# New planner constants for the issue order of a fused attention and MLP kernel on one core

## The chip, the cores and the metric

The kernel runs on one core of a Trainium2 chip. Its engines are TensorE (PE in the profile, its weight loads PEld), VectorE (DVE), ScalarE (ACT), GpSimd (POOL) and SyncE (SP), which only issues DMA transfers here. The metric is the device time of one execution in microseconds, lower is better. A run is one timed execution; the median of three is given.

## The reference

Causal attention in a window of 128 positions, with a linear bias per head, over 8 batches of 576 positions with 8 heads of 64; then an MLP with a rational activation on the 4608 x 512 result. All inputs are f32, but the two weight matrices of the MLP are float64.

```
scores = q @ k.T / 8 - slope[h] * (i - j)   where 0 <= i - j < 128, else -1e9
x = softmax(scores) @ v                     # (4608, 512)
h = x @ w_in                                # (4608, 2048), w_in and w_out are float64
g = (a0 + a1 h + a2 h^2 + a3 h^3) / (1 + |b0| |h| + |b1| h^2 + 1e-6)
out = g @ w_out                             # (4608, 512)
```

## The kernel before

The 4608 rows are cut into 36 blocks of 128, and these into 18 tiles of two blocks. For each tile there are two attention jobs `j` (tile `j // 2`, four heads each), so 36 jobs. A job's PE block holds the value matmuls of the job before it and its own scores: `attention(j)` emits `values(j - 1)` and `scores` as one step from job 3 on. After the scores come, for each of two head pairs, a predicated copy that folds the band (line 491), bias and minimum (532), exponentials (537), sums and reciprocals (544, 545), the scaling (546, on GpSimd), a transposition (on PE at 561 for the first six jobs, by a DMA transposition at line 568 with ScalarE copies at 566 and 569 on either side for the others), and two GpSimd steps on the far part (589, 590; the first jobs have VectorE and ScalarE steps at 580 to 582 in their place). `out_values` then makes `x_hi` and `x_lo`, the two parts of the MLP's input.

The MLP of a tile, `mlp(t, cs)`, runs over 16 chunks `c` of 128 hidden units, two at a time: up-projection into PSUM `h` (line 667), the rational function on ScalarE, GpSimd and VectorE (lines 681 to 707), and the down-projection into two accumulators (line 724), which also wait for the tile before to be copied out (752). Tiles 1 to 17 multiply with weights and inputs split into a high and a low part, three matmuls for each product. Tile 0 multiplies with unsplit f32 weights.

The weights arrive as 64-bit words. `convert(k)` loads a chunk of 512 KB of `w_in` (even k) or `w_out` (odd k), and turns it into f32 in three steps (628 on ScalarE, 629 on ScalarE or VectorE, 630 on VectorE). `split(c, m)` makes the high part on ScalarE (642) and the low part on GpSimd or VectorE (643), when the loads that share the high part's memory have been converted. PSUM has four buffers with the tag `h`, which the up-projections, the score blocks' sides and the conversions share.

No step is issued where it stands in the source. Each is handed to `Plan.op` with a due time, a cost per engine it can run on, its reads and writes, and perhaps a time `after` which the plan may place it. `Plan.order` goes through a planned time line: whenever an engine is free in the plan, it takes from the steps that are ready there the one with the lowest due time. The sequence in which steps are taken is then the order of the instructions on each engine and on SP's DMA queue. On the chip an engine only follows its sequence and waits on semaphores; due times, costs and `after` have no effect there other than through the order. `LATENCY` and the slack (SP, SV, SA, SG, in us for PE, VectorE, ScalarE and GpSimd) lengthen planned waits between engines. A step marked `sb` is planned to exclude such steps between VectorE and GpSimd.

The due times come from some 40 constants:

- `m_time(t, c)`: the up-projection of a chunk. Tile 0 starts at T0 and lasts L0, later blocks last L1 each. Down-projections are due ML later (LL more in the last tile), elementwise steps ME later.
- `a_time(j)`: jobs 0 and 1 at A0 and A0 + 4 DA; job 2 at B2, job 3 at B3; later ones at `m0 + (j % 2 + AOFF) * (m1 - m0) * ZA / 2`, where m0 and m1 are the starts of the tile before and of the job's own. Loads of kq are due JL before, those of v VL after kq; AW is how much ahead the plan may place them. V0, D0, D2, D4, DU, BL and DL shift steps within a job, VE the v loads of the first jobs.
- `c_time(k)`: conversions, C0 + DC c for w_in and CO + DO c for w_out; the load is due WL before.
- splits: S0 + DS (2c + m), in the plan not before SL ahead of that.
- FE ends the PE's warming matmuls (line 760) that fill its idle time at the start. OE shifts the output copy.

Of the kernel before, what the change touches and what calls it, by code (L numbers as in the profile page):

```python
# [16 lines left out]
U16 = mybir.dt.uint16  # L17
# [4 lines left out]
P = 128  # L22
# [259 lines left out]
def banded_attention_ratio_mlp(ctx: ExitStack, tc: tile.TileContext, kqv, w_in, w_out, ab, bias, ident, out):  # L282
    nc = tc.nc
# [10 lines left out]
    NJ = 2 * NTILE  # L294


    A0, DA, T0, L0, L1 = -20.125, 1.042, 19.836, 59.132, 26.846
    AOFF, D2, D3, JL, VL = -0.9676, 4.293, 7.221, 11.472, 6.149
    SP, SV, SA, SG, LL = 0.000768, 0.2712, 0.1218, 0.4427, 2.857
    ML, ZA, ME, OE, C0 = 24.839, 1.199, 1.338, 10.451, 0.4053  # L300
    DC, CO, DO, WL, S0 = 3.813, 18.57, 3.877, 4.536, 80.884
    DS, SL, AW, BL, VE = 1.477, 8.756, 26.824, 0.9349, 13.143
    DU, V0, DL, B2, B3 = 0.7375, 2.733, 1.877, 23.544, 56.47
    FE, D0, D4 = 19.023, 0.5665, 1.663

    plan = Plan({"p": 1000 * SP, "v": 1000 * SV, "a": 1000 * SA, "g": 1000 * SG})

    def slot(pool, shape, dtype, name, tag=None, view=None):
        return Slot(pool, count[id(pool)], shape, dtype, name, tag or name, view)

    def ap(s):
        if s.ap is None:
            s.ap = s.pool.tile(s.shape, s.dtype, name=s.name, tag=s.tag)
        return s.ap

    def act(n, psum, ptr=0):
        return (67 if psum else 105) + 0.833 * n + 95 * ptr

    def dve(n, ptr=0):
        return 69 + 1.042 * n + 60 * ptr  # L320
# [42 lines left out]
    def a_time(j):  # L363

        t = j // 2
        if t == 0:
            return A0 + 4 * DA * j
        if t == 1:
            return B2 if j == 2 else B3
        m0, m1 = m_time(t - 1, 0), m_time(t, 0)  # L370
        return m0 + (j % 2 + AOFF) * (m1 - m0) * ZA / 2
# [5 lines left out]
    def job(j, i):  # L377

        t, p = j // 2, 2 * (j % 2) + i
        W = tile_width(2)  # L380
        N = 5 * P
        u0 = a_time(j) + i * DL
        o = (t * NPAIR + p) * P * W
        src = kqv[o : o + P * W].rearrange("(q w) -> q w", w=W)
        kq = slot(sb4, [P, 5 * P], F32, "kq")
        v = slot(sb6, [P, 2, 2, P], F32, "v")
        late = 0.0 if t == 0 else 1000 * (u0 - AW)

        def load_v(e, b):
            part = src[:, N + b * P : N + (b + 2) * P]  # L390
            eng[e].dma_start(ap(v)[64 * b : 64 * b + 64].rearrange("r g j c -> r g (j c)"), part.rearrange("(g r) w -> r g w", g=2))

        plan.op(u0 - JL if t else 2 * j + i - 19, {"s": 1150}, lambda e: eng[e].dma_start(ap(kq), src[:, :N]), writes=[(kq, 0)], after=late)
        for b in range(2):
            plan.op(u0 - JL + VL if t else 2 * j + i - VE, {"s": 560}, lambda e, b=b: load_v(e, b), writes=[(v, b)], after=late, rows=0.5)
        kt = lambda b: ap(kq)[:, b * P : (b + 2) * P]
        qt = lambda b: ap(kq)[:, (3 + b) * P : (4 + b) * P]
        return kt, qt, v, [(kq, 0)]
# [40 lines left out]
    def attention(j):  # L439

        A = a_time(j)
        t = j // 2
        back = j - 1 if j > 2 else None
        if j != 1:
            shared[:] = [slot(ps4, [P, 2, 2, P], F32, f"side{h}", tag="h") for h in range(2)]
        side, n = list(shared), 1 if j == 1 else 0
        if j == 1:
            banks = [slot(ps1, [P, 2, 2, P], F32, f"sc{h}", tag=f"acc{h}") for h in range(2)]
            main, mk = (lambda h: ap(banks[h])), [(banks[0], 0), (banks[1], 0)]
        elif j < NJ:  # L450
            sc = slot(ps1, [P, 2, 2, 2, P], F32, "sc")
            main, mk = (lambda h: ap(sc)[:, h]), [(sc, 0), (sc, 1)]
        extra = lambda h: ap(side[h])[:, n].rearrange("q i (b c) -> q i b c", b=2)
        if j < NJ:
            jobs = [job(j, i) for i in range(2)]

        def scores(i):
            kt, qt = jobs[i][:2]
            for b in range(2):
                for part in range(2):  # L460
                    for g in range(2):
                        for h in range(2):
                            r, c = slice(64 * h, 64 * h + 64), slice(64 * g, 64 * g + 64)
                            k0 = P * g if part == 0 else P - 64 * g
                            to = extra(h)[c, i, b] if part else main(h)[c, i, b]
                            nc.tensor.matmul(to, qt(b)[r, c], kt(b)[r, k0 : k0 + (64 if part else P)], start=True, stop=True, tile_position=(64 * h, 64 * g))  # L466

        beside = lambda b: ap(side[b])[:, 1]
        if t == 0:
            for i in range(2):  # L470
                plan.op(A + DU * i, {"p": 290 + 664}, lambda e, i=i: scores(i), reads=jobs[i][3], writes=mk + [(side[0], n), (side[1], n)], rows=0.9)
        else:
            small, reads, writes, cost = [], [], [], 290
            if back is not None:
                small.append(values(back, beside))
                reads += stage[back, 0][1] + stage[back, 1][1]
                writes += [(side[0], 1), (side[1], 1)]
                cost += 2 * 664 + 53
            if j < NJ:
                small += [lambda: scores(0), lambda: scores(1)]  # L480
                reads += jobs[0][3] + jobs[1][3]
                writes += mk + [(side[0], 0), (side[1], 0)]
                cost += 2 * 664
            plan.op(A, {"p": cost}, lambda e: [f() for f in small], reads=reads, writes=writes, rows=0.9)
            if back is not None:
                out_values(back, A, beside, lambda b: (side[b], 1))
        if j >= NJ:
            return

        for h in range(2):  # L490
            plan.op(A + 0.5, {"v": dve(4 * P)}, lambda e, h=h: nc.vector.copy_predicated(  # L491
                out=main(h).rearrange("q i b (k c) -> q (i b) k c", k=2),
                mask=halves(ap(masks)[:, 0].bitcast(U32))[:, None].to_broadcast([P, 4, 2, 64]),
                data=extra(h).rearrange("q i b c -> q (i b) c")[:, :, None].to_broadcast([P, 4, 2, 64])),
                reads=[mk[h], (side[h], n), (masks, 0)], writes=[mk[h]])
        for i in range(2):
            unit(j, i, A + DU * i, main, mk, None if t == 0 else (lambda i=i: ap(sc)[:, :, i]), jobs[i][2])
        if t == 0:
            if j == 0:
                sums[:] = [slot(ps1, [P, 2, 2, 2, P], F32, "px", tag="sc")]  # L500
            px = sums[0]
            run = values(j, lambda b: ap(px)[:, b, j])
            plan.op(A + V0, {"p": 290 + 53 + 2 * 664}, lambda e: run(), reads=stage[j, 0][1] + stage[j, 1][1], writes=[(px, 2 * j), (px, 2 * j + 1)], rows=0.9)
            out_values(j, A + V0, lambda b: ap(px)[:, b, j], lambda b: (px, 2 * j + b))
# [3 lines left out]
    def unit(j, i, A, main, mk, pt, v):  # L508
# [30 lines left out]
        for h in range(2):  # L539
            for b in range(2):  # L540
# [6 lines left out]
                reads=[(pr, y) for y in range(4)] + [(st, 12)], writes=[(pr, y) for y in range(4)], sb=True)  # L547

        w = slot(sb3, [P, 4 * P], F32, "p_all")
# [13 lines left out]
        if j >= TURNED:  # L563
            planes = slot(sb2, [P, 2, 4 * P], U16, "planes")
            turned = slot(sb2, [P, 8, P], U16, "turned")
            plan.op(A + 1.4, {"a": act(8 * P, 0)}, lambda e: nc.scalar.copy(ap(planes), ap(pr).rearrange("q k y c -> q (k y c)").bitcast(U16).rearrange("q (x s) -> q s x", s=2)),
                    reads=[(pr, y) for y in range(4)], writes=[(planes, 0)])
            plan.op(A + D4, {"s": 1300}, lambda e: eng[e].dma_start_transpose(ap(turned), ap(planes).rearrange("q s x -> q (s x)")), reads=[(planes, 0)], writes=[(turned, 0)])
            plan.op(A + D2 + 0.2, {"a": act(8 * P, 0)}, lambda e: nc.scalar.copy(ap(w)[:, : 4 * P].bitcast(U16).rearrange("q (x s) -> q s x", s=2), ap(turned).rearrange("q (s g) x -> q s (g x)", s=2)),
                    reads=[(turned, 0)], writes=[(w, 0)])  # L570
        else:
            plan.op(A + (D2 if t else D0), {"p": 28 + 108 * 4}, transpose, reads=[(pr, y) for y in range(4)] + [(id_sb, 0)], writes=pk)
# [15 lines left out]
        cost = {"g": 190 + 2.08 * 256}  # L588
# [241 lines left out]
```

## Time and profile before

| | |
|---|---|
| runs | 976.63, 977.81, 979.15 us; median 977.81 |
| span of the profiled execution, first to last instruction | 977.0 us, which lies within the runs; no other time is given for it |
| instructions | 25,069 |
| mean TensorE clock granted | 0.997 of full speed |
| mean DMA traffic | 92 GB/s |

Idle time of an engine that sets no end costs nothing. Matmuls are pipelined and their ends are modelled, so a PE that is always busy is not PE at its peak. A wait is ascribed to what was released last.

### The profile page before, as it was taken

The page shows a single profiled execution, that of the slowest core. Times are in us where ns is not written, and L with a number is a line of the kernel's source. Part 1 is how long each engine was busy: PE and PEld are TensorE (multiplying, and loading weights), DVE is VectorE, ACT ScalarE, POOL GpSimd, SP SyncE. Part 2 cuts the span into 40 slices and gives each one's busy share as a digit, 9 for nine tenths or more (in the row PEclk, how much of TensorE's full clock was granted, in tenths as well). Part 3 has the DMA queues.
Part 4 walks back from the last instruction along what each step waited for, and adds up shares of the span by engine and source line. Part 5 has one row for each costly group of instructions (what it writes and reads, how often), then busy time and mean ns, then how long its engine had stood idle before and what let it go on. Part 6 is the DMA issues. An engine that isn't in the chain of part 4 may idle for free. (4 is left out here: it accounts for less than half of the span.)

```text
span 977.0 us, 25069 instructions
## 1 busy us (share of the span) xinstructions
PE 957.9 (98%) x9838; PEld 846.8 (87%) x9838; DVE 780.3 (80%) x1803; ACT 704.0 (72%) x1482; POOL 500.3 (51%) x502
## 2 busy tenths in 40 slices
PE   9898999999999999999999999999999999999998
PEld 7665888899999999999898989989899999999997
DVE  6799888877788878787887778877887788878776
ACT  5888877777677777777767777777777776777653
POOL 0327774555455554555555545545555545554542
PEclk9999999999999999999999999999999999999999
DMA  8991213333333332232332333433222332321100
GB/s 277 363 337 53 77 46 91 79 77 93 78 88 81 89 77 84 70 98 78 82 80 52 71 103 77 93 77 77 71 71 78 77 84 64 92 72 45 23 22 21
DMA packets 117861, 89.57 MB, mean 92 GB/s; under 512 B 68848, under 2 KB 101872, under 8 KB 117744
## 3 DMA queue, kind: packets, MB, share of 16 engines
q1 hardware_dynamic: 117744, 87.98, 33.0%
q8 instruction: 77, 1.26, 0.6%
q14 instruction: 40, 0.33, 0.1%
HBM read 62.79 MB, written 9.44 MB: 74 GB/s over the span
## 5 line engine op out<-in xcount | busy, mean ns | idle before, releaser
L667 PE MATMUL h<-x_hi,hi 128*128 128x256 f32 x1088 | 308.5, 284 | 1.5 <-DVE x_lo L436 1.5
L667 PE MATMUL h<-x_lo,hi 128*128 128x256 f32 x1088 | 306.4, 282 | 0.0
L667 PE MATMUL h<-x_hi,lo 128*128 128x256 f32 x1088 | 306.2, 281 | 0.0
L667 PEld LDWEIGHTS h<-x_lo,hi 128*128 128x128 f32 x1088 | 205.3, 189 | 31.4 <-issue 0.7
L667 PEld LDWEIGHTS h<-x_hi,hi 128*128 128x128 f32 x1088 | 205.6, 189 | 20.7 <-issue 3.3
L724 PE MATMUL acc<-hi,g_h 128*128 128x512 f32 x544 | 215.5, 396 | 1.4 <-ACT o L752 1.4
L724 PE MATMUL acc<-lo,g_h 128*128 128x512 f32 x544 | 214.8, 395 | 0.0
L667 PEld LDWEIGHTS h<-x_hi,lo 128*128 128x128 f32 x1088 | 205.6, 189 | 0.0
L724 PE MATMUL acc<-hi,g_l 128*128 128x512 f32 x544 | 198.0, 399 | 1.3 <-DVE g_l L707 1.2
L683 POOL TENSOR_SCALAR g_q<-g_u,babs 128x512 f32<-128x512 f32 x136 | 107.5, 791 | 168.5 <-ACT g_u L681 157.6
L546 POOL TENSOR_TENSOR pr<-pr,st 128x512 f32<-128x512 f32 x70 | 78.7, 1127 | 221.2 <-DVE st L545 131.5
L698 POOL TENSOR_TENSOR g_q<-g_q,g_u 128x512 f32<-128x512 f32 x136 | 178.2, 1311 | 19.9 <-ACT g_q L683 10.8
L704 DVE SCALAR_TENSOR_TENSOR g_h<-h,ab_sb,g_u 128x512 fp32r<-128x512 f32 x136 | 101.4, 746 | 68.7 <-ACT g_u L702 68.3
L699 DVE TENSOR_TENSOR g_p<-h,g_p 128x512 f32<-128x512 f32 x136 | 93.5, 688 | 64.1 <-ACT g_p L697 50.3
L681 ACT ACTIVATE g_u<-h 128x512 f32<-128x512 f32 x144 | 86.1, 598 | 77.4 <-PE h L667 45.6
L537 ACT ACTIVATE pr<-pr,st 128x128 f32<-128x128 f32 x288 | 111.9, 391 | 39.8 <-DVE st L532 39.7
L697 ACT ACTIVATE g_p<-h,ab_sb 128x512 f32<-128x512 f32 x136 | 105.7, 779 | 45.0 <-PE h L667 44.7
L701 ACT ACTIVATE g_u<-g_q,fixed 128x512 f32<-128x512 f32 x136 | 98.3, 724 | 44.1 <-POOL g_q L698 43.9
L700 DVE SCALAR_TENSOR_TENSOR h<-g_p,ab_sb,h 128x512 f32<-128x512 f32 x136 | 102.3, 752 | 19.7 <-ACT g_u L681 17.8
L724 PEld LDWEIGHTS acc<-hi,g_h 128*128 128x128 f32 x544 | 102.6, 189 | 9.6 <-ACT o L752 1.8
L705 DVE SCALAR_TENSOR_TENSOR g_q<-g_q,g_h 128x512 f32<-128x512 f32 x136 | 105.9, 780 | 5.7
L724 PEld LDWEIGHTS acc<-hi,g_l 128*128 128x128 f32 x544 | 100.3, 188 | 11.1 <-DVE g_l L707 2.2
(82 smaller groups left out, 1561.6 us busy)
## 6 DMA issues: line engine op xcount, KB each, us to landing
kq<-in_kqv SPq DMA_DIRECT2D x72, 320.0 KB, 3.6
v<-in_kqv SPq DMA_DIRECT2D x144, 128.0 KB, 3.8
out<-o SPq DMA_DIRECT2D x34, 256.0 KB, 2.0
raw<-in_w_in SPq DMA_DIRECT2D x16, 512.0 KB, 8.5
raw<-in_w_out SPq DMA_DIRECT2D x16, 512.0 KB, 8.7
bias_t<-in_bias SPq DMA_DIRECT2D x44, 64.0 KB, 2.8
turned<-planes SPq DMA_TRANSPOSE x60, 3.1
out<-o SPq DMA_DIRECT2D x4, 128.0 KB, 1.7
```

The costliest lines, as they stand in the source:

```text
L537: nc.scalar.activation(ap(pr)[:, :, y, :], ap(pr)[:, :, y, :], AF.Exp, bias=ap(st)[:, y : y + 1], scale=-1.0, accum_out=ap(st)[:, 4 + y : ...
L667: nc.tensor.matmul(h(n), w[:, k, :], x[:, k, :], start=(k == 0 and m == 0), stop=(k == NKC - 1 and m == len(seq) - 1))
L681: plan.op(E, {"a": act(W, 1)}, lambda e: nc.scalar.activation(v(g_u), v(h_s), AF.Abs), reads=[(h_s, 0)], writes=[(g_u, 0)])
L683: lambda e: nc.scalar.activation(v(g_q), v(g_u), AF.Identity, bias=ap(babs)[:, 0:1], scale=ap(babs)[:, 1:2]) if e == "a" else nc.gpsimd.te ...
L697: plan.op(E, {"a": act(W, 1, 2) - 20}, lambda e: nc.scalar.activation(v(g_p), v(h_s), AF.Identity, bias=ap(ab_sb)[:, 2:3], scale=ap(ab_sb) ...
L698: plan.op(E, {"g": ttc}, lambda e: nc.gpsimd.tensor_tensor(v(g_q), v(g_q), v(g_u), ALU.mult), reads=[(g_q, 0), (g_u, 0)], writes=[(g_q, 0) ...
L699: plan.op(E, {"v": dve(W)}, lambda e: nc.vector.tensor_tensor(v(g_p), v(h_s), v(g_p), ALU.mult), reads=[(h_s, 0), (g_p, 0)], writes=[(g_p, ...
L700: plan.op(E, {"v": dve(W, 1)}, lambda e: stt(v(h_s), v(g_p), ap(ab_sb)[:, 1:2], v(h_s), ALU.add, ALU.mult), reads=[(h_s, 0), (g_p, 0), (ab ...
L701: plan.op(E, {"a": act(W, 0, 1)}, lambda e: nc.scalar.activation(v(g_u), v(g_q), AF.Ln, bias=guard, scale=1.0), reads=[(g_q, 0)], writes=[ ...
L704: plan.op(E, {"v": dve(W, 1)}, lambda e: stt(v(g_h), v(h_s), ap(ab_sb)[:, 0:1], v(g_u), ALU.add, ALU.mult), reads=[(h_s, 0), (g_u, 0), (ab ...
L705: plan.op(E, {"v": dve(W)}, lambda e: stt(v(g_q), v(g_q), GUARD, v(g_h).bitcast(F32), ALU.add, ALU.mult), reads=[(g_q, 0), (g_h, 0)], writ ...
L724: nc.tensor.matmul(ap(accs[t][i]), x[:, sl], w, start=(c == 0 and part == 0 and m == 0), stop=(c == NFC - 1 and part == parts - 1 and m == ...
```

## The change

Nearly all constants get new values, and the costs of three steps in the plan change: the fixed part of the PE block with values and scores, the predicated copy, and the ScalarE copy of turned probabilities. The steps themselves, their number, their operands and their possible engines stay.

```diff
--- before.py
+++ after.py
@@ -294,14 +294,14 @@
     NJ = 2 * NTILE
 
 
-    A0, DA, T0, L0, L1 = -20.125, 1.042, 19.836, 59.132, 26.846
-    AOFF, D2, D3, JL, VL = -0.9676, 4.293, 7.221, 11.472, 6.149
-    SP, SV, SA, SG, LL = 0.000768, 0.2712, 0.1218, 0.4427, 2.857
-    ML, ZA, ME, OE, C0 = 24.839, 1.199, 1.338, 10.451, 0.4053
-    DC, CO, DO, WL, S0 = 3.813, 18.57, 3.877, 4.536, 80.884
-    DS, SL, AW, BL, VE = 1.477, 8.756, 26.824, 0.9349, 13.143
-    DU, V0, DL, B2, B3 = 0.7375, 2.733, 1.877, 23.544, 56.47
-    FE, D0, D4 = 19.023, 0.5665, 1.663
+    A0, DA, T0, L0, L1 = -47.434, -4.4983, 20.199, 59.889, 26.027
+    AOFF, D2, D3, JL, VL = -0.59154, 2.043, 9.3559, 11.43, 4.2802
+    SP, SV, SA, SG, LL = 0.094693, 0.089416, 0.04452, 0.39081, 9.8968
+    ML, ZA, ME, OE, C0 = 24.177, 1.2512, 2.8928, 6.8434, 2.5163
+    DC, CO, DO, WL, S0 = 4.2374, 7.2467, 5.7357, 5.1523, 74.675
+    DS, SL, AW, BL, VE = 1.6055, 17.867, 100.24, -0.66684, 9.7087
+    DU, V0, DL, B2, B3 = 0.19073, 2.8395, 0.36831, 23.177, 43.982
+    FE, D0, D4 = 19.392, 2.008, -3.928
 
     plan = Plan({"p": 1000 * SP, "v": 1000 * SV, "a": 1000 * SA, "g": 1000 * SG})
 
@@ -470,7 +470,7 @@
             for i in range(2):
                 plan.op(A + DU * i, {"p": 290 + 664}, lambda e, i=i: scores(i), reads=jobs[i][3], writes=mk + [(side[0], n), (side[1], n)], rows=0.9)
         else:
-            small, reads, writes, cost = [], [], [], 290
+            small, reads, writes, cost = [], [], [], 220
             if back is not None:
                 small.append(values(back, beside))
                 reads += stage[back, 0][1] + stage[back, 1][1]
@@ -488,7 +488,7 @@
             return
 
         for h in range(2):
-            plan.op(A + 0.5, {"v": dve(4 * P)}, lambda e, h=h: nc.vector.copy_predicated(
+            plan.op(A + 0.5, {"v": dve(4 * P) + 118}, lambda e, h=h: nc.vector.copy_predicated(
                 out=main(h).rearrange("q i b (k c) -> q (i b) k c", k=2),
                 mask=halves(ap(masks)[:, 0].bitcast(U32))[:, None].to_broadcast([P, 4, 2, 64]),
                 data=extra(h).rearrange("q i b c -> q (i b) c")[:, :, None].to_broadcast([P, 4, 2, 64])),
@@ -566,7 +566,7 @@
             plan.op(A + 1.4, {"a": act(8 * P, 0)}, lambda e: nc.scalar.copy(ap(planes), ap(pr).rearrange("q k y c -> q (k y c)").bitcast(U16).rearrange("q (x s) -> q s x", s=2)),
                     reads=[(pr, y) for y in range(4)], writes=[(planes, 0)])
             plan.op(A + D4, {"s": 1300}, lambda e: eng[e].dma_start_transpose(ap(turned), ap(planes).rearrange("q s x -> q (s x)")), reads=[(planes, 0)], writes=[(turned, 0)])
-            plan.op(A + D2 + 0.2, {"a": act(8 * P, 0)}, lambda e: nc.scalar.copy(ap(w)[:, : 4 * P].bitcast(U16).rearrange("q (x s) -> q s x", s=2), ap(turned).rearrange("q (s g) x -> q s (g x)", s=2)),
+            plan.op(A + D2 + 0.2, {"a": act(8 * P, 0) + 265}, lambda e: nc.scalar.copy(ap(w)[:, : 4 * P].bitcast(U16).rearrange("q (x s) -> q s x", s=2), ap(turned).rearrange("q (s g) x -> q s (g x)", s=2)),
                     reads=[(turned, 0)], writes=[(w, 0)])
         else:
             plan.op(A + (D2 if t else D0), {"p": 28 + 108 * 4}, transpose, reads=[(pr, y) for y in range(4)] + [(id_sb, 0)], writes=pk)
```

## Rows read from the trace of the kernel before

**Rows 1.** The page, busy times of the engines over the span.

```profile
PE 957.9 (98%) x9838; PEld 846.8 (87%) x9838; DVE 780.3 (80%) x1803; ACT 704.0 (72%) x1482; POOL 500.3 (51%) x502
```

**Rows 2.** Windows: length; busy us and count by engine; then PEclk, DMA share, GB/s.

```profile
20.80:40.00 19.20, 16.78 (x190) 13.91 (x191) 12.90 (x31) 14.72 (x31) 5.43 (x6) 1.00 1.07 353
40.00:60.00 20.00, 16.72 (x53) 9.60 (x52) 19.40 (x43) 18.98 (x38) 5.29 (x6) 0.91 1.06 366
60.00:82.00 22.00, 22.00 (x200) 15.63 (x199) 21.61 (x52) 19.91 (x43) 8.45 (x9) 1.00 0.77 245
82.00:98.00 16.00, 12.89 (x156) 7.66 (x155) 14.75 (x26) 12.21 (x28) 14.35 (x12) 0.89 0.09 24
...
110.00:160.00 50.00, 46.93 (x517) 41.41 (x516) 44.64 (x98) 37.72 (x89) 29.03 (x25) 1.00 0.20 64
160.00:961.00 801.00, 799.19 (x8304) 723.73 (x8303) 636.85 (x1457) 575.57 (x1182) 424.78 (x433) 1.00 0.30 74
961.00:977.00 16.00, 12.05 (x55) 9.58 (x53) 8.01 (x13) 3.89 (x7) 2.07 (x2) 1.00 0.09 33
```

**Rows 3.** The chain that ended last: start, length, what.

```profile
738.54 1.50 PE side L417 x64
...
763.63 1.50 PE side L417 x64
...
917.03 1.50 PE side L417 x64
```

**Rows 4.** VectorE in order of time: start, length, step, idle time before it.

```profile
49.73 0.42 DVE L582 TENSOR_TENSOR p_far<-sc,masks 128x256 f32<-128x256 f32 x1 [0.44 <-ACT p_all L580]
...
85.39 1.05 DVE L544 TENSOR_TENSOR st<-st,fixed 128x4 f32<-128x4 f32 x1
```

**Rows 5.** PE in order of time.

```profile
34.53 5.42 PE L667 MATMUL h<-x_hi,w 128*128 128x256 f32 x24 [1.20 <-DVE w L630]
...
68.60 0.67 PE L417 MATMUL side<-p_all,v 64*64 64x128 f32 x16
...
88.29 0.66 PE L561 MATMUL sc<-id_sb,pr 128*128 128x128 f32 x4 [1.67 <-POOL pr L546]
90.39 2.08 PE L724 MATMUL acc<-w,g 128*128 128x512 f32 x2 [1.44 <-DVE g L695]
92.39 1.13 PE L417 MATMUL side<-p_all,v 64*64 64x128 f32 x16
...
98.11 0.68 PE L667 MATMUL h<-x_hi,hi 128*128 128x256 f32 x1
```

**Rows 6.** Two lines: duration in ns, minimum, median and maximum.

```profile
L491 DVE COPY_PREDICATED sc<-masks,side x72: 679/689/697, 6.9 to 896.6; 128x512 f32<-128x512 uint32 x72
...
L569 ACT COPY p_all<-turned x60: 1345/1362/1388, 163.7 to 910.7; 128x1024 uint16<-128x1024 uint16 x60
```

**Rows 7.** SP's DMA issues in order of time: start, length.

```profile
12.73 2.84 SPq L623 DMA_DIRECT2D raw<-in_w_in  x5
...
47.75 0.33 SPq L393 DMA_DIRECT2D kq<-in_kqv  x1
...
52.06 0.33 SPq L393 DMA_DIRECT2D kq<-in_kqv  x1
```

**Rows 8.** ScalarE in order of time, first conversion steps of two chunks.

```profile
23.60 0.70 ACT L628 ACTIVATE raw<-raw 128x512 f32<-128x512 f32 x1
...
33.03 0.67 ACT L628 ACTIVATE raw<-raw 128x512 f32<-128x512 f32 x1 [0.81 <-DMA raw<-in_w_in]
```

**Rows 9.** GpSimd in order of time, last step of a job.

```profile
759.59 1.08 POOL L590 TENSOR_TENSOR p_all<-p_all,p_far 128x256 f32<-128x256 f32 x1
```

**Rows 10.** Three lines: duration in ns, minimum, median and maximum.

```profile
L544 DVE TENSOR_TENSOR st<-st,fixed x72: 132/153/1055, 11.3 to 903.0; 128x4 f32<-128x4 f32 x72
...
L643 POOL TENSOR_TENSOR lo<-w,hi x24: 1268/1284/1743, 78.7 to 131.1; 128x512 fp32r<-128x512 f32 x24
...
L643 DVE TENSOR_TENSOR lo<-w,hi x8: 660/840/1681, 90.9 to 126.1; 128x512 fp32r<-128x512 f32 x8
```

## The prediction

> **What bounds the kernel now.** I read the page's busy times first, then the span cut into stretches, then TensorE (PE) in order of time, and last the chain that ended last. PE is busy 957.9 us [rows 1], so all other orders of the same work can gain at most what PE loses, and the stretches say where that is [rows 2]. From 160 to 961 us PE is busy 799.19 of 801 us at full clock. There the work itself is the bound: the 64-matmul value blocks follow one another every 25.5 us, seven intervals from 738.54 to 917.03 [rows 3], one per half tile, and PE has 1.8 us of gaps in all. After 961 us PE is busy 12.05 us more, with the last down-projections, and the final store follows.
>
> The losses lie before 160 us. Up to 20.8 us come the first loads and attention jobs 0 and 1. Then, as idle time plus half the time at the lower of the two clock levels (1.2 of 2.4 GHz; a mean of 0.91 is 18% of the time at half, 0.89 is 22%): 20.8 to 40 us 2.4 idle; 40 to 60 us 3.3 idle and 1.8 by the clock; 82 to 98 us 3.1 idle and 1.8 by the clock; 110 to 160 us 3.1 idle [rows 2]. That is 15.5 us. What limits these stretches is not PE: DMA is full (share above 1) from 20.8 to 60 us while weights come in, VectorE is 97 to 98% busy from 40 to 82 us and ScalarE 95% from 40 to 60 us.
>
> The hole at 82 to 98 us has one visible cause. Attention job 2 was ready to give its values at 50.1 us (its last far part starts at 49.73 and takes 0.41) [rows 4], but the block with its values and job 3's scores came at 68.60 [rows 5]. Job 3's chain then ended with two PE waits: transposes at 88.29 that waited 1.67 us for GpSimd, and its values at 92.39. Tile 1's up-projections, which read them, start at 98.11. Between them PE waited 1.44 us for tile 0's elementwise work and ran two down matmuls in 2.08 us at the lower clock [rows 5].
>
> **The change, part by part.** No instruction is added or removed; the planner's constants put the same ones into another order on every engine and on the DMA queue of SP. Due times below are worked out by the formulas in the code; they rank what is ready, and are no forecast of time.
>
> *Three durations.* The plan's PE block goes from 290 to 220 ns of fixed part, the predicated copy from 602 to 720 ns, the ScalarE copy of the turned probabilities from 958 to 1,223 ns. The trace has 689 and 1,362 ns [rows 6]. On the chip nothing changes in length. What they can mend, a consumer queued too early, costs PE at most the 1.8 us of gaps after 160 us. I take 0; bounds 0 and -1.8.
>
> *Job 3 earlier.* Its due time (B3) falls from 56.5 to 44.0, that of its two kq loads from 45.0 to 32.6. These loads were issued at 47.75 and 52.06 [rows 7]. In units of a 512 KB weight chunk, 28.8 units stood in the queue up to the second one; now 18.5. At 353 GB/s [rows 2] a unit takes 1.49 us, so it is issued about 15 us earlier, at some 37 us, and the block waits only for job 2's values (50.1 us). It can run at 50 to 55 us in place of 68.6, if the elementwise chain of job 3 is given VectorE and ScalarE. Job 4's dues go the other way (47.8 to 60.8, its loads 36.4 to 49.4) but that job can't run before job 3's values, which in the trace are at 92.39. So values of job 3 at about 75 to 80 us, and tile 1's up-projections are no longer short of data at 82 us. Worth 0 to 4.9 us (all of the hole); I take 4.0, since VectorE's load remains.
>
> *Splits earlier.* The 32 splits of weights into high and low part are due from 74.7 (was 80.9), the last at 124.4 (was 126.7), and may be planned from 56.8 us (was 72.1). The losses of 110 to 160 us, 3.1 us, lie where the splits and tile 1's first elementwise work share GpSimd and VectorE. Worth between 0 and 3.1; I take 1.0, because the last one moves by only 2.3 us.
>
> *Output weights spread.* The w_out conversions go from 18.6 + 3.88c to 7.2 + 5.74c: the first 11 us earlier, the last 16.6 later (93.3). The late ones belong to the end of tile 0, whose downs ran beside tile 1's ups until past 98 us anyway, so later costs nothing while other PE work is ready. But the early ones push w_in loads back: the fifth by 4.25 units (6.3 us), the sixth by 3 (4.5 us), the seventh by 2.5 (3.7 us). The fifth's first conversion step was at 23.60 [rows 8]; plus 6.3 and 2.1 for three steps like this one of 0.70 makes 32.0, ahead of the matmuls at 34.53 [rows 5]. The seventh's was at 33.03; plus 3.7 and 2.1 makes 38.8, and PE wants it after 16 of the 24 matmuls that begin at 34.53 and take 5.42 us, at 38.1. So 0.7 us late: I take a loss of 1.0, bounds 0 and 6.3 (a delay that goes through in full).
>
> *First jobs, order of 0 and 1.* Job 1 now ranks ahead of job 0 (-65 against -47), v loads 3.4 us later in rank; all still rank ahead of the first weight load, which was issued after the eight v loads at 12.73 [rows 7]. Both jobs' values are needed before chunk 0 is complete, so the order between them is taken as 0, bounds -1 and +1.
>
> *Steady state.* Attention is due 19.3 us ahead of the tile before for even jobs (31.2 before), and 13.3 us behind its start for odd ones (1.0 before). The chain is already tight: a job's last GpSimd step ends at 760.67 [rows 9] and its values run at 763.63 [rows 3], 3.0 us later. Its ops keep ranking ahead of the elementwise work then at hand, since the block of an odd job runs about 25 us into that tile. I take 0. Load gates (AW) and the last tile's due times (LL) change no PE work: 0.
>
> *Sum.* -4.0 - 1.0 + 1.0 = -4.0 on the profiled span of 977.0, so 973.0. The runs' median of 977.8 lies 0.8 above that span, so I predict **973.8 us**.
>
> **A rule that speaks against it.** A step on VectorE that is 153 ns in the median took 1,055 ns at 85.39 us, beside GpSimd's splits; VectorE's own splits go from 660 to 1,681 ns [rows 4, 10]. The Trainium skill, page "SBUF — State Buffer", section "Who interferes with whom", says that a VectorE instruction with two SBUF inputs and a GpSimd instruction that reads SBUF exclude each other: whichever comes second waits until the first has ended. The trace agrees (1,055 against 153 ns). By it, splits moved forward would take VectorE's time just where it is short; this is rival 2, 984.6 us where the sum says 973.8.
>
> **Rivals.** (0) The forecast: the hole closes. Own range 968 to 975; chance 0.48.
>
> (1) No change: the hole only moves. For: VectorE is 97% busy from 40 to 82 us, and what job 3 takes earlier, conversions and tile 0's elementwise work lose; PE then waits for them instead. Against: it is idle 1.25 us in 82 to 98 us and a third of 20.8 to 40 us. Price: the 4 us are given back between 55 and 98 us; 975 to 981, chance 0.30.
>
> (2) Slower: splits on GpSimd collide with a full VectorE before 82 us. Each collision costs up to 0.9 us (1,055 less 153). Four splits rank earlier by the shift alone (6.2 us at 1.6 us each), sixteen could run if GpSimd starts at 57 us (21 us at 1.28 us each). Four cost 3.6 us, sixteen 14 us, if PE waits for all of it. Against the sum's gain of 4.0 it decides from eight collisions on (7.2 us, 981.0); twelve give 973.8 + 10.8 = 984.6 us. Against: a split needs both its weights converted and ScalarE's high part first, and ScalarE is 19.91 of 22 us busy from 60 to 82 us. Chance 0.12.
>
> (3) Slower: the attention chain slips in the steady state. If odd jobs fall behind elementwise work by more than the 3.0 us of slack, what lies beyond is paid in 16 tiles: half a microsecond makes 8 us, 982 us, and 0.45 decides; a full one makes 990. For: the 12 us later rank. Against: the rank margin above. Chance 0.10.
>
> **How the numbers follow.** About 0.3% (3 us) is what measurement can tell from no change here: faster is below 974.9, slower above 980.7. Case 0 is mostly faster, its upper end just not, and case 1 leaks a little to both sides; 2 and 3 are slower. So faster 0.47, same 0.31, slower 0.22. The low end of the range is all of the hole, all of 110 to 160 us and half of the rest of the gaps: 977.8 - 4.9 - 3.1 - 2.8 = 967. The high end takes in rival 2 at eleven collisions and rival 3 up to 0.6 us a tile: 984.
>
> **What would show it.** Right: the block with job 3's scores at 50 to 58 us, tile 1's first steady ups before 90 us, clock 1.00 at 82 to 98 us, and from 160 us on the same 25.5 us period, shifted some 4 us earlier. Wrong: a new PE gap at 30 to 60 us on a conversion; VectorE steps several times their median beside splits before 80 us; a period above 25.6 us or gaps well above 1.8 us after 160 us.

## The result, and the profile after

The changed kernel takes 968.69 us (median of four runs, 967.79 to 969.15) and the kernel before 977.22 (976.05 to 979.15): a ratio of 0.9902, 95% interval 0.9882 to 0.9922. It is 8.5 us faster where the forecast was 4.0 (973.8 us, range 967 to 984). The profiled execution took 969.15 us with a span of 967.4; before, the span was 977.0. The 9.6 us between the spans are what the profile has to explain.

First the page of the changed kernel, PE's busy time.

```profile
PE 957.1 (99%) x9846; PEld 844.9 (87%) x9846; DVE 792.5 (82%) x1798; ACT 701.8 (73%) x1485; POOL 492.8 (51%) x504
```

PE's idle time falls from 977.0 - 957.9 = 19.1 us [rows 1] to 967.4 - 957.1 = 10.3. So 8.8 of the 9.6 us are idle time of PE that is gone. The eight matmuls more are warming matmuls (L760, 94 and 102 of them in the traces): by these the number of steps does change.

The same stretches as in [rows 2] for the changed kernel: length; busy us and count of PE, PEld, DVE, ACT, POOL; then PEclk, DMA share, GB/s. The stretch of 98 to 110 us is new here; before, PE was busy 12.00 of its 12 us. Each such row is of one execution.

```profile
20.80:40.00 19.20, 17.90 (x220) 14.16 (x213) 15.47 (x37) 15.97 (x35) 3.91 (x5) 1.00 1.07 369
40.00:60.00 20.00, 17.57 (x173) 10.40 (x172) 18.56 (x47) 19.41 (x41) 7.62 (x7) 1.00 1.08 325
60.00:82.00 22.00, 22.00 (x199) 14.83 (x198) 21.13 (x46) 21.28 (x51) 13.73 (x13) 1.00 0.82 249
82.00:98.00 16.00, 16.00 (x86) 11.98 (x85) 15.43 (x43) 15.83 (x40) 13.87 (x12) 1.00 0.38 101
98.00:110.00 12.00, 10.95 (x166) 8.04 (x165) 10.99 (x15) 10.22 (x19) 8.76 (x7) 1.00 0.13 47
110.00:160.00 50.00, 50.00 (x436) 45.43 (x435) 44.65 (x96) 41.42 (x90) 35.73 (x32) 1.00 0.23 62
160.00:952.00 792.00, 791.25 (x8253) 714.62 (x8252) 645.91 (x1448) 564.10 (x1171) 405.05 (x424) 1.00 0.29 75
952.00:967.40 15.40, 11.45 (x50) 9.01 (x48) 8.15 (x13) 2.70 (x5) 2.58 (x2) 0.94 0.10 34
```

The reader is to compare PE's busy time with the length, stretch by stretch, and then the clock. The hole at 82 to 98 us is closed: 16.00 of 16 at full clock, where it was 12.89 at 0.89. From 110 to 160 us PE is never idle (46.93 before). From 20.8 to 60 us the idle time goes from 5.7 to 3.7 us, and the clock stays at 1.00 where it was 0.91 from 40 to 60. One loss is new, 1.05 us at 98 to 110. From 160 us on there was little to gain, and the gaps go from 1.8 to 0.8 us. The losses from 20.8 to 160 us, 15.5 us by the count of the prediction, are 1.3 + 2.4 + 1.05 = 4.8 now. The last stretch holds 3.95 us of idle time in both kernels, but its clock is 0.94 where it was 1.00 before: some 0.9 us lost by the same count.

PE of the changed kernel in order of time, the rows that answer to [rows 5].

```profile
41.10 3.70 PE L724 MATMUL acc<-w,g 128*128 128x512 f32 x8 [0.52 <-DVE g L695]
...
49.17 3.70 PE L724 MATMUL acc<-w,g 128*128 128x512 f32 x8 [1.40 <-DVE g L695]
52.80 0.69 PE L417 MATMUL side<-p_all,v 64*64 64x128 f32 x14
...
75.48 0.67 PE L417 MATMUL side<-p_all,v 64*64 64x128 f32 x16
...
83.86 0.47 PE L667 MATMUL h<-x_hi,hi 128*128 128x256 f32 x1
```

The step with job 2's values and job 3's scores runs at 52.80 us (68.60 before), job 3's values at 75.48 (92.39 before). What that opens is seen in the up-projection's line alone, here for 82 to 98 us: PE busy us (count), PEld, clock, DMA share, GB/s. First the kernel before, then the changed one.

```profile
82.00:98.00 16.00, 1.19 (x9) 0.94 (x7) 0.89 0.09 24
```

```profile
82.00:98.00 16.00, 12.46 (x63) 9.64 (x64) 1.00 0.38 101
```

Before, nine up matmuls ran in this stretch, now 63. Of these, 16 read `x_lo`, which only tile 1 has here (2 before), and each stands with two others of tile 1; so about 48 of the 63 are tile 1's up-projections, and the rest are the last of tile 0. Job 3's kq loads on SP's queue, which were at 47.75 and 52.06 [rows 7]:

```profile
32.19 2.31 SPq L393 DMA_DIRECT2D kq<-in_kqv  x2
```

The steady state in the chain that ended last, the first and the last of the same eight value blocks as in [rows 3]:

```profile
730.30 1.50 PE side L417 x64
...
907.98 1.50 PE side L417 x64
```

Seven intervals make 177.68 us, 25.38 each, against 25.50. That this is no gain per tile is seen in the output copies on ScalarE. Tile 1's, before and after:

```profile
168.64 1.07 ACT L752 COPY o<-acc 128x512 f32<-128x512 f32 x2
```

```profile
159.22 1.06 ACT L752 COPY o<-acc 128x512 f32<-128x512 f32 x2
```

They come 9.4 us earlier. Tile 16's come at 926.43 against 936.01, 9.6 us earlier. So all of the gain is there when tile 1 ends, and 15 tiles on it has hardly changed. The account nearly fits: up to 160 us PE is busy 154.44 us against 146.69, 7.8 more; the lower clock cost 3.6 before and nothing now; eight more warming matmuls (14.85 us in all against 13.69) do no work. 7.8 + 3.6 - 1.2 = 10.2 us of work more, for tile 1's copies that come 9.4 us earlier. The 3.6 us are an estimate from rounded mean clocks.

### The profile page after: what moved, and what is told of

The parts are those of the page before. It is cut to its first block, busy times and chain, and to the rows that moved or that the text cites. A ratio compares the mean times of both kernels' runs of the same rounds, so it can differ in the third digit from the quotient of the medians.

```text
span 967.4 us, 25085 instructions
## 1 busy us (share of the span) xinstructions
PE 957.1 (99%) x9846; PEld 844.9 (87%) x9846; DVE 792.5 (82%) x1798; ACT 701.8 (73%) x1485; POOL 492.8 (51%) x504
## 4 chain that ended last, share of the span: by engine, by line
PE 92%; DVE 3%; ACT 3%; DMA 1%; issue 1%; DVEq 0%
PE h L667 41%; PE acc L724 40%; PE side L417 5%; PE sc L466 3%; PE side L466 2%; PE warm L760 1%; DMA turned<-planes 1%; ACT g_u L681 0%; ACT g_p L697 0%; ACT raw L628 0%; DVE g_h L704 0%; PE sc L561 0%; DVE g_p L699 0%; DVE g_q L705 0%; ACT g_u L702 0%
## 5 line engine op out<-in xcount | busy, mean ns | idle before, releaser
L724 PE MATMUL acc<-hi,g_l 128*128 128x512 f32 x544 | 194.8, 398 | 0.0
L546 POOL TENSOR_TENSOR pr<-pr,st 128x512 f32<-128x512 f32 x69 | 72.6, 1052 | 224.7 <-DVE st L545 100.8
L697 ACT ACTIVATE g_p<-h,ab_sb 128x512 f32<-128x512 f32 x136 | 103.2, 777 | 47.3 <-PE h L667 46.8
L724 PEld LDWEIGHTS acc<-lo,g_h 128*128 128x128 f32 x544 | 102.1, 188 | 9.5
```

The source lines that it names most:

```text
L697: plan.op(E, {"a": act(W, 1, 2) - 20}, lambda e: nc.scalar.activation(v(g_p), v(h_s), AF.Identity, bias=ap(ab_sb)[:, 2:3], scale=ap(ab_sb) ...
L724: nc.tensor.matmul(ap(accs[t][i]), x[:, sl], w, start=(c == 0 and part == 0 and m == 0), stop=(c == NFC - 1 and part == parts - 1 and m == ...
```

## The experiments

e1 to e4 and e7 have four runs each, the others ten, all beside the kernel before, which had a median of 978.1 to 978.3 us on each of the three chips that were used. In all, the order no longer comes from the plan on the spot but from a list: step by number (-1 is a warming matmul) and engine.

```diff
-    order = plan.order()
+    order = [(plan.ops[i].emit if i >= 0 else warming, e) for i, e in ORDER]
     with tc.manual_schedule():
-        for o in order:
-            o.emit(o.engine)
+        for emit, e in order:
+            emit(e)
```

So an experiment can change the order of a part alone. Where constants are exchanged, the plan is made anew with them; its order is taken for the steps that it starts before 160 us, and all later steps stand in the old order. A line of constants moves the line numbers up by one in e5 to e11.

**e1: the new start, the old rest.** The list holds the steps that the changed kernel's plan starts before 160 us in its order, and all others in the order of before.

> The new order for every step that the plan starts before 160 us, the old order for all steps that are left. Theory (the whole gain is made in the first 160 us): 968.7 us give or take 1.5, as the changed kernel. Rival (the new due times of the steady state have a share): 971 us or more, with PE gaps after 160 us above the 0.75 us that the changed kernel shows there.

969.35 us, ratio 0.9905 [0.9879, 0.9932]. Its windows (columns as above):

```profile
110.00:160.00 50.00, 50.00 (x436) 45.43 (x435) 44.65 (x96) 41.43 (x90) 36.20 (x32) 1.00 0.24 64
...
160.00:952.00 792.00, 791.98 (x8261) 717.20 (x8261) 630.35 (x1449) 567.49 (x1172) 417.54 (x426) 1.00 0.29 75
```

The whole gain is in the first 160 us. The new order of the steady state is worth nothing that can be measured, and the old one joined to the new start costs nothing either. That makes e1 the mark for the runs below, which have the old rest too. e1 also shows how far one execution's stretches can be trusted: with the changed kernel's start it has PE busy 16.79 us at 20.8 to 40 us, 1.1 less than there.

**e2, e3, e4: one group moved by itself.** The edit is the list alone: one kernel's steps sorted by their planned start, with the steps of one group given the other plan's start and engine. e2 is the changed kernel with jobs 3 to 5 at their old times, e3 the kernel before with jobs 3 to 5 and tile 1's MLP at their new times, e4 the kernel before with the weights' loads and conversions at their new times.

> The new order, with all steps of attention jobs 3, 4 and 5, their loads among them, put back to the plan times of the old one (some 15 us later); the rest as in the new order, tile 1's up-projections right after the values that they read. Theory (job 3 earlier is what closes the hole at 82 to 98 us): about 4.9 us of PE loss come back, 973 to 975 us, with idle PE and a lower clock between 75 and 98 us. Rival (job 3 had nothing to do with it, the splits or the weights had): within 1.5 us of 968.7.

> The old order, with the steps of attention jobs 3, 4 and 5 and of tile 1's MLP at the plan times of the new one; weights, splits and all else as in the old order. Theory (the hole closes): 972 to 973 us, the stretch 82 to 98 us full at clock 1.00. Rival (VectorE and ScalarE are full there, so the wait only moves to the conversions): 976 to 979 us, with new PE gaps at 55 to 80 us.

> The old order, with all loads and conversions of weights at the plan times of the new one. The prediction's step (w_out spread costs about 1 us, as w_in comes later): 977 to 979 us. Rival (the earlier w_out conversions are what took 2.8 us of loss out of 40 to 60 us and 1.1 out of 20 to 40 us): 973 to 975 us, with a clock of 1.00 at 40 to 60 us.

All are far slower than both kernels: e2 997.95 us, 1.0196 [1.0166, 1.0226], 28.6 us above e1; e3 1000.41, 1.0229 [1.0199, 1.0260]; e4 991.54, 1.0134 [1.0109, 1.0159]. One row of each: PE in order of time in e2, a window of e3, and the group of PE's waits in e4 (us in total, times, longest).

```profile
86.88 1.12 PE L561 MATMUL sc<-id_sb,pr 128*128 128x128 f32 x4 [6.06 <-POOL pr L546]
```

```profile
60.00:82.00 22.00, 16.72 (x49) 9.82 (x48) 19.08 (x50) 16.66 (x40) 6.11 (x6) 0.85 0.88 274
```

```profile
PE h L667 <- DVE w L630: 12.0, 5, 4.0
```

When one group is moved alone, steps that are not ready stand in a queue ahead of work that is, and all behind them waits: PE 6.06 us for GpSimd in e2, 12.0 us for conversions in e4 (3.0 in the kernel before). None of the forecasts held, and these runs don't tell the theories apart. They show that a group moved in a fixed order is no test of what the planner does with its constant: it moves everything else as well. The runs that follow therefore change constants and plan anew.

**e5: only job 3's due time new.**

```diff
+    B3 = 43.982
```

> The old constants with the new due time of job 3 alone (B3 43.982), planned anew; steps that this plan starts before 160 us in its order, all later ones in the old order. Unlike a plain move, all other steps find new places around job 3. Theory (job 3 earlier closes the hole at 82 to 98 us by itself): 972 to 974.5 us, values of job 3 some 8 us or more ahead of 92.4. Rival (it needs the other constants too; the loss only goes elsewhere before 160 us): 976 to 980 us.

978.80 us, 1.0005 [0.9992, 1.0018]: no change. Windows, and PE in order of time:

```profile
40.00:60.00 20.00, 15.54 (x42) 7.51 (x40) 19.32 (x42) 19.05 (x39) 6.47 (x7) 0.85 1.08 317
...
82.00:98.00 16.00, 16.00 (x186) 11.48 (x185) 14.58 (x33) 15.07 (x35) 14.92 (x13) 1.00 0.27 83
```

```profile
43.57 4.54 PE L725 MATMUL acc<-w,g 128*128 128x512 f32 x6 [2.02 <-DVE g L696]
```

The hole at 82 to 98 us is closed, as the forecast has it, and the time is the same. Job 3's scores came at 60.18, its values at 86.18. The loss of 40 to 60 us grew (4.46 idle, and a clock of 0.85), that of 20.8 to 40 as well (15.62 busy). This is the prediction's rival 1, the hole that only moves, though not to where the rival had it (55 to 98 us): by the prediction's count the 4.9 us come back as 3.5 us more loss at 20.8 to 60 us and some 1.9 at 60 to 110.

**e6: only job 3's due time old**, all else as in the changed kernel.

```diff
+    B3 = 56.47
```

> The new constants with the old due time of job 3 (B3 56.47), planned anew, spliced in the same way. Theory (job 3 is the cause): values of job 3 fall back to about 90 us and the hole opens again, 4 to 7 us over the changed kernel, 973 to 976 us. Rival: within 1.5 us of 969.

977.61 us, 0.9991 [0.9975, 1.0006]: the whole gain is lost.

```profile
82.00:98.00 16.00, 12.88 (x158) 8.06 (x157) 14.53 (x22) 13.59 (x27) 13.97 (x12) 0.89 0.01 2
```

The hole is back, nearly to the digit of [rows 2], with job 3's values at 93.8 us. So job 3's early time is needed, and e5 says that it does not suffice. Of the 8.3 us above e1 the hole holds 4.9; PE is idle 1.1 us more at 60 to 82 us and 1.9 more at 110 to 160, so job 3's time costs something there as well.

**e7: only the splits old.**

```diff
+    S0, DS, SL = 80.884, 1.477, 8.756
```

> The new constants with the old ones of the splits (S0, DS, SL), planned anew, spliced in the same way. By the prediction's step (splits earlier are worth 1.0, at most 3.1 us): 969 to 972 us, job 3's values still at about 75 us and the loss at 98 to 160 us. Rival (the splits carry the hole as well, since tile 1's first matmuls need both): 973 us or more.

972.14 us, 0.9932 [0.9915, 0.9948]: 2.8 us above e1.

```profile
110.00:160.00 50.00, 48.75 (x427) 44.17 (x427) 41.43 (x95) 38.78 (x86) 35.32 (x30) 1.00 0.23 62
```

PE's idle time of 110 to 160 us returns in part (1.25 us), with 0.52 at 82 to 98; job 3's values stay early (74.81 us).

**e8 and e9: the weights' times old in the changed kernel, and new in the kernel before.**

```diff
+    C0, DC, CO, DO, WL = 0.4053, 3.813, 18.57, 3.877, 4.536
```

```diff
+    C0, DC, CO, DO, WL = 2.5163, 4.2374, 7.2467, 5.7357, 5.1523
```

> The new constants with the old ones of loads and conversions of weights (C0, DC, CO, DO, WL), planned anew, spliced in the same way. By the prediction's step (the spread of w_out costs 1 us): 967 to 969 us. Rival (the spread makes room for job 3 on VectorE and ScalarE, and it earns the gain at 20 to 60 us): 972 to 976 us, job 3's block later than 55 us.

> The old constants with the new ones of loads and conversions of weights alone, planned anew, spliced as before (later steps in the old order). After four runs the theory is that job 3 and the weights have to move together: alone 976 to 980 us, like job 3 alone. Rival (the weights carry the gain, job 3 only uses it): 970 to 974 us.

e8 976.72 us, 0.9990 [0.9973, 1.0006], nearly all of the gain gone; e9 976.30, 0.9972 [0.9960, 0.9984], 1.9 us gained by the medians, 1.6 to 3.9 by the interval. One window and one row of PE of e8, then of e9:

```profile
40.00:60.00 20.00, 16.17 (x66) 9.14 (x68) 19.09 (x44) 18.97 (x39) 6.20 (x6) 1.00 1.06 373
```

```profile
57.75 1.98 PE L725 MATMUL acc<-w,g 128*128 128x512 f32 x4 [2.37 <-DVE g L696]
```

```profile
40.00:60.00 20.00, 16.86 (x167) 11.31 (x171) 18.13 (x40) 17.07 (x36) 6.20 (x6) 1.00 1.08 310
```

```profile
41.44 1.99 PE L725 MATMUL acc<-w,g 128*128 128x512 f32 x4 [2.74 <-DVE g L696]
```

With the old times PE waits 2.37 us for tile 0's elementwise work at 55 us, and job 3's step slips to 59.67 (52.80 in the changed kernel). Both runs have the new spread on the faster side, where the prediction had it cost 1.0 us. But most of this lies elsewhere than at 20.8 to 60 us, where the prediction looked. PE's idle time in e8 is 2.1 us more than in the changed kernel there, and 3.8 more at 82 to 160 us (1.0 and 4.2 against e1). e9 gains under 1 us at 20.8 to 60, but 3.3 of the 4.9 us of the hole:

```profile
82.00:98.00 16.00, 14.44 (x179) 9.93 (x179) 14.84 (x34) 15.58 (x35) 13.61 (x12) 1.00 0.25 75
```

So the weights' times alone close two thirds of it, with job 3's values no earlier than 89.59 us: early values of job 3 are not all that can fill it.

**e10 and e11: more of the new constants in the old set.** e10 has job 3's time and the weights' times; e11 the constants that act in the start alone. The three durations and the slack stay old in e11, and so do the constants that act in the start and later: ML, ME, D2, DL, JL, VL, BL and AW, and AOFF and ZA, which time jobs 4 and 5.

```diff
+    B3 = 43.982
+    C0, DC, CO, DO, WL = 2.5163, 4.2374, 7.2467, 5.7357, 5.1523
```

```diff
+    B3, B2, C0, DC, CO, DO, WL, S0, DS, SL, A0, DA, D0, V0, VE, DU, FE, T0, L0 = 43.982, 23.177, 2.5163, 4.2374, 7.2467, 5.7357, 5.1523, 74.675, 1.6055, 17.867, -47.434, -4.4983, 2.008, 2.8395, 9.7087, 0.19073, 19.392, 20.199, 59.889
```

> The old constants with both the new due time of job 3 and the new ones of the weights, planned anew and spliced. Theory (the pair is enough): 969 to 973 us, the hole at 82 to 98 us closed and the loss at 20 to 60 us no larger than in the old order. Rival (each constant is worth something only in its own set): 975 us or more.

> The old constants with all new ones of the start (jobs 0 to 3, weights, splits, tile 0), planned anew and spliced; slack, the three durations and the constants of later tiles as in the old kernel. Theory (the constants of the start make the gain): 968 to 971 us. Rival (they fit only with the durations and the slack they were planned with): 973 us or more.

e10 979.53 us, 1.0011 [0.9999, 1.0024]; it had 4.95 us of PE idle time from 160 to 560 us, behind the seam, where some of the later steps do not stand in the old order, so its time is only partly that of its start. e11 975.06, 0.9971 [0.9960, 0.9982]: 3.1 us by the medians, a third of the gain, and by the ratio no more than e9. Its rival came true, but what is missing can be the durations, the slack or the constants that act in both. A window of e11:

```profile
40.00:60.00 20.00, 16.46 (x169) 9.70 (x169) 19.39 (x43) 16.88 (x36) 6.32 (x7) 1.00 1.07 305
```

Its step with job 3's scores comes at 53.63, almost as early as in the changed kernel, but the values at 82.92: 29.3 us behind it in place of 22.7.

**e12: only the three durations old**, the other constants new.

```diff
-            small, reads, writes, cost = [], [], [], 220
+            small, reads, writes, cost = [], [], [], 290
-            plan.op(A + 0.5, {"v": dve(4 * P) + 118}, lambda e, h=h: nc.vector.copy_predicated(
+            plan.op(A + 0.5, {"v": dve(4 * P)}, lambda e, h=h: nc.vector.copy_predicated(
...
-            plan.op(A + D2 + 0.2, {"a": act(8 * P, 0) + 265}, ...
+            plan.op(A + D2 + 0.2, {"a": act(8 * P, 0)}, ...
```

> The new constants with the three old durations, planned anew and spliced. The prediction's step (the durations are worth 0 to 1.8 us): 969 to 971 us. Rival (a plan with durations that differ from the chip's puts steps of the start in a worse order): 973 us or more, with PE waits for conversions or elementwise work before 160 us.

980.07 us, 1.0017 [1.0002, 1.0032]: 10.7 us above e1, the whole gain lost and a little more. Windows, and PE in order of time:

```profile
60.00:82.00 22.00, 16.83 (x72) 11.91 (x70) 21.66 (x53) 21.53 (x50) 15.58 (x13) 0.99 0.80 251
82.00:98.00 16.00, 14.41 (x167) 10.95 (x168) 15.86 (x32) 14.05 (x32) 14.23 (x13) 0.90 0.28 83
```

```profile
82.18 0.90 PE L417 MATMUL side<-p_all,v 64*64 64x128 f32 x10 [3.60 <-issue]
```

The longest idle time in one stretch of all the planned starts, 5.2 us, lies at 60 to 82 us, where neither kernel has any. PE stands 3.60 us in the middle of job 3's values. The profile names no releaser, but a VectorE step ends at 82.08, 0.10 us before PE goes on:

```profile
81.39 0.69 DVE L695 SCALAR_TENSOR_TENSOR g<-g_q,h 128x512 f32<-128x512 f32 x1
```

It is the last to read a buffer `h` of tile 0, and the values' second block needs one of these four buffers. So the wait is likely one for a buffer that the plan had counted on earlier.

**All planned starts beside each other.** Where the step with job 3's scores and where job 3's values begin (PE in order of time), and the median:

| order | scores, us | values, us | median, us |
|---|---|---|---|
| e7, old splits | 52.1 | 74.8 | 972.14 |
| after | 52.8 | 75.5 | 968.69 |
| e1 | 53.3 | 76.0 | 969.35 |
| e12, old durations | 55.0 | 78.1, most of it 82.2 | 980.07 |
| e8, old weights | 59.7 | 82.6 | 976.72 |
| e11, constants of the start alone | 53.6 | 82.9 | 975.06 |
| e10, job 3 and weights | 57.3 | 83.9 | 979.53 |
| e5, job 3 alone | 60.2 | 86.2 | 978.80 |
| e9, weights alone | 57.6 | 89.6 | 976.30 |
| before | 68.6 | 92.4 | 977.22 |
| e6, old job 3 | 62.1 | 93.8 | 977.61 |

The three orders whose values of job 3 begin by 76 us (e1 and the changed kernel have the same start) are the three below 973. Among the others the values' start does not order the times: what it gives in the hole is lost elsewhere.

## Why the prediction came out as it did

**What bounds the kernel: right.** The loss lay before 160 us, and e1 shows that all of the gain does too.

**Job 3 earlier, -4.0: right in mechanism and size at its place.** The loads were issued at 32.19 us (forecast 37), the step ran at 52.80 (50 to 55), the values at 75.48 (75 to 80). The stretch of 82 to 98 us gave all of its 4.9 us. e6 shows the need for it. But the term was written as if it stood on its own, and e5 shows that it does not: with the other constants old, rival 1 is what happens. The sum came out because the other parts paid what rival 1 would have taken. Nor is job 3 the hole's one cause, as the prediction had it: in e9 most of the hole closes with job 3's due time old and its values at 89.59 us.

**Output weights spread, +1.0: this is the step that failed, by its sign.** It had the spread cost 1.0 us through a seventh chunk that comes 0.7 us late. In fact the stretches of 20.8 to 60 us, where it would be felt, lost 3.7 us in place of 7.5, so 3.8 were gained (2.7 by e1's trace). Not all of that is the weights': e8, with their old times, loses 5.9 there. PE's waits for tile 0's elementwise work (first line) and for conversions (second) before 160 us, first in the changed kernel, then in the kernel before (us in total, times, longest):

```profile
PE acc L724 <- DVE g L695: 1.9, 2, 1.4
PE h L667 <- DVE w L630: 1.2, 3, 0.6
```

```profile
PE acc L724 <- DVE g L695: 3.4, 2, 2.0
PE h L667 <- DVE w L630: 3.0, 4, 1.3
```

The wait for conversions, which the step was afraid of, got shorter. e8 and e9 show the sign from both sides, 7.4 and 1.9 us. The working looked at when a chunk comes, and called what is put off free; it did not ask what the queue of a full engine gains when work is put off. That this is the mechanism is a guess: VectorE's conversion steps from 20 to 82 us fall from 26.7 to 22.1 us, but e9 gains with 26.9, and most of the price of e8 lies behind 82 us. The sign is shown, its cause stays open.

**Splits earlier, -1.0: too small.** The stretch of 110 to 160 us lost nothing any more, the whole bound of 3.1, less 1.05 that is new at 98 to 110. e7 puts 2.8 us on it. The last split's due time, on which the small value was based, said little about the stretch.

**Three durations, 0 with a bound of 1.8: failed as a bound, not seen in the sum.** The step allowed the durations an effect only on late consumers in the steady state. e12 shows 10.7 us, in the start: with other durations the planner takes the steps in another sequence, and the new constants give their gain only with the new durations. Whether it matters that these lie nearer to the chip's for the two copies, or only that they belong to this set, no run shows.

**The sum.** The undone parts cost 8.3 (e6), 7.4 (e8), 2.8 (e7) and 10.7 us (e12) against e1, 29 in all for a gain of 8.5. Added alone to the old set they give 0 (e5) and 1.9 (e9), and those of the start alone 3.1 (e11). So no part has a share of the gain that could be added to another's; the prediction's sum over parts had the right sign and half of the size. That the time fell into the range is partly luck. The term that made up the forecast, job 3, is worth nothing by itself, and what made it count was forecast as a loss (weights), as 1.0 of 2.8 us (splits) and as nothing (durations). The low end of the range, 967 us, was taken from the stretches, and it is what kept the measured time inside. Taken by stretch rather than by constant there is an account: 3.8 us at 20.8 to 60, 4.9 at 82 to 98, 2.0 at 98 to 160, 1.1 behind. That is 11.8, some 2 more than the spans' 9.6; 1.2 of it go into warming matmuls, some 0.9 into the lower clock of the last stretch, and the clock's part is worked out from rounded means.

**What the plan itself says.** The prediction went by due times and rightly called them no forecast. But `Plan.order` also gives every step a planned start, which follows from the code alone. The planned time line ends at 966.4 us with the kernel before and at 959.0 with the changed one, 7.4 us earlier where the chip gains 8.5. It has the step with job 3's scores at 66.4 and 51.7 us and job 3's values at 88.7 and 73.6; the chip has 68.60 and 52.80, 92.39 and 75.48. With one part of the new set old, the whole plan (the runs have the old rest in its place) ends later than either kernel's: 993.2 us (job 3), 985.9 (weights), 977.3 (splits), 981.7 (durations). So the plan told the gain, and that the parts don't add. These are times of the plan and not of the chip, and they don't rank the four undone parts as the chip does.

**First jobs 0, steady state 0.** The steady state is right (e1), but that the last tile's due times change nothing is not quite: the last stretch's clock is 0.94, and 1.00 in e1, which has the old rest. The first jobs were not undone by themselves.

**Rivals.** 1 did not happen in the change as a whole, but did in e5. 2 did not: from 60 to 82 us six splits ran instead of three, one of them on VectorE for 1.36 us (660 ns at the least [rows 10]), and PE was busy 22.00 of 22. 3 did not: the gaps from 160 us on fell.

**The signs.** The step with the scores, the clock and the period told rightly. "Tile 1's first steady ups before 90 us" told nothing: the kernel before has a first small group of them at 81.70, which the prediction, with its 98.11, had passed over. The count in the stretch, 63 against 9, is what tells.

**Left open:** how much of each undone part's price is that part's own, and how much the planner's new sequence of everything else; and the slack and the constants that act in both the start and later (ML, ME, D2 and others), which no run changed alone.

## What to carry to other kernels

With a planned order, cost the stretches and not the constants: say how much each stretch can give and whether the new order frees the engine that is full there, since a constant's effect can be nothing in one set and 8 us in another. Read the planned starts and not the due times. When work moves, ask what its old place gains as well as what its new place loses. And undo a part by planning anew, never by moving a group through fixed queues, which cost 13 to 29 us here whichever group it was.

## What was not expected of the hardware

**Collisions that cost nothing.** VectorE is busier than before, 792.5 against 780.3 us, with the same work. The sums of the softmax (line 544), from 160 to 950 us (count, busy us, mean ns), first in the changed kernel, then in e1 with the old order there:

```profile
L544 DVE TENSOR_TENSOR st<-st,fixed 128x4 f32<-128x4 f32 x58 | 22.5, 388 | 0.0
```

```profile
L544 DVE TENSOR_TENSOR st<-st,fixed 128x4 f32<-128x4 f32 x58 | 9.1, 157 | 0.0
```

The step is 2.5 times as long on average. In the changed kernel 26 of the 58 take over 0.3 us, and each of these ends within 0.1 us of the end of a GpSimd step; in e1 none takes as long. One of them in order of time, and what GpSimd did then, in the changed kernel:

```profile
404.80 0.69 DVE L544 TENSOR_TENSOR st<-st,fixed 128x4 f32<-128x4 f32 x1
```

```profile
404.43 1.04 POOL L546 TENSOR_TENSOR pr<-pr,st 128x512 f32<-128x512 f32 x1 [6.69 <-ACT pr L537]
```

The VectorE step ends at 405.49, 0.02 us behind GpSimd's at 405.47. The Trainium skill, page "SBUF — State Buffer", section "Who interferes with whom", has the two engines exclude each other on a shared port, and this agrees. But 13.4 us of such waiting change nothing in the time (968.69 against 969.35 us): PE is the bound there, and VectorE is busy 82% of the time.

**The clock after short gaps.** In the kernel before and in e5 PE was idle 1.98 and 2.02 us at 40 to 44 us, each time soon after 24 up matmuls that had themselves waited (1.20 and 1.70 us), and the six down matmuls that came next took 4.54 us; eight take 3.70 at full clock. The row of the kernel before:

```profile
42.37 4.54 PE L724 MATMUL acc<-w,g 128*128 128x512 f32 x6 [1.98 <-DVE g L695]
```

The stretch's granted clock was 0.91 and 0.85. In e9 a gap of 2.74 us at the same place, behind waits of 1.11 and 0.71 us, left four down matmuls at 1.99 us, and the clock of the stretch at 1.00. So the length of the last gap alone does not tell which of the two levels, 1.2 or 2.4 GHz, comes next.
